# Attention and squared-ReLU MLP in one kernel: weights loaded and split earlier, two staging pools for the bias rows, and the exponent's offset computed on ScalarE

## The chip, the cores and the metric

The kernel runs on one core of a Trainium2 chip. A core has five engines, each with an instruction queue of its own that it works through in order: TensorE (PE, matmuls; its weight loads are listed as PEld), VectorE (DVE), ScalarE (ACT), GpSimd (POOL) and SyncE (SP). In this kernel every DMA is issued by SP, so SP's queue (SPq in the rows) is the order in which transfers start. The metric is device time in microseconds: the median of three runs, and, for the profile, one profiled execution.

## What is computed

```python
scores = scale * np.matmul(q, k.transpose(0, 1, 3, 2))          # 4 batches, 8 heads, 576 rows, 64 wide
x = (psi_rel / psi_i)[..., None]                                # log1p(|i-j|) / log1p(max(i,1))
h = np.maximum(x @ w1 + b1, 0.0)                                # 32 hidden values
bias = h @ w2                                                   # one value a head, the same for all batches
scores = scores + bias.transpose(2, 0, 1)[None, :, :, :]
scores = scores - np.max(scores, axis=-1, keepdims=True)
attn = np.exp(scores)
attn = attn / (np.sum(attn, axis=-1, keepdims=True) + 1e-09)
out = np.matmul(attn, v)
...
h = np.maximum(x @ w_in, 0.0)                                   # 2304 tokens, 512 -> 2048
return (h * h @ w_out).astype(np.float32)                       # 2048 -> 512
```

## The kernel before

**Number format.** Matmul operands are fp16 pairs: a value is split into a high half and the remainder, and a product is three matmuls (high by high, high by low, low by high). A split costs a cast of the high half and a subtraction for the low one, on ACT, POOL or DVE as the table `ENG` (L30) says.

**Steps.** The attention is 80 steps: two batch pairs, five row chunks of each (`ORDER`, L39), eight heads of each chunk. Chunk 0 of a pair holds the last 64 rows of both batches (one softmax block of 128 rows a step), the others 128 rows of both (two blocks a step). The first two chunks, steps 0 to 15, are done with fp32 transposes on PE and an fp32 product with v (`f32c`, L129); from step 16 on, the exponentials are split on ACT and POOL and transposed by DMA. Step t does `qk` (scores into the PSUM tile `sc`), `softmax_a`, `softmax_b`, and, three steps late, `pv`. The softmax of a block is: DVE adds the bias tile `bt` to `sc` and takes the row maximum (`s`, `mx`, L382); DVE makes the exponent's offset `nm` = ESC ln 2 - max (L385, 128x1); ACT takes the exponential with `nm` as its bias and sums the row (L388).

**The bias** depends on the rows, not on the batch, so it is made once, in 36 groups of 16 rows: four rows `hg` a group and quadrant of hidden values (L278 on ACT or L281 on DVE; the string `HID` and the list `PATS` say how many of a group's four are made on ACT), a matmul with w2 (`bp`, L308), an eviction `be` (L319 or L321), a DMA of `be` into a DRAM table `biasd` (L323), and for each step a DMA of its bias tile `bt` back (L336, L338; three buffers). `be` takes one of five buffers of the pool `r_p`, which `cv` (below) and, from step 11 on, the MLP's `r` and output tiles use as well. Four groups are made before step 0, the others a group or two a step. The groups of the second chunk, steps 8 to 15, are numbers 16 to 23, the fifth to twelfth that are made.

**The MLP's weights** are 32 loads of 512 KB (`WT`, L178). Each goes to one of three staging buffers `stg`, is rounded to fp32 by three DVE instructions (`ci` L200, `ci` L201, `cv` L203), cast on ACT (`winH`, `woutH`, L121) and finished by two POOL instructions. I call the whole a weight task. The loads of k share the staging buffers; k and v of the first pair and the weight tasks stand in one list `loads`, where `W_AT` (L38) says how many weight tasks follow each head's k and v; a step takes its share from the list: it splits the oldest load and starts the next.

**The MLP** runs in units of 256 hidden values (`g1`: 24 matmuls `hp`, L506; `g2`: 12 matmuls into `o`, L529) as soon as a chunk's attention is finished (`finish_x`), one unit a step and the rest after the last step.

**What sets the order.** The program is traced in the order of `for t in range(NS + LAG)` (L672) and then reordered by a list scheduler by priorities; `with later(n)` (L595) lowers the priority of what is traced inside. Each engine then runs its own fixed list and waits on semaphores.

## Time and profile before

| | us |
|---|---|
| runs | 711.01, 713.51, 713.33 (median 713.33) |
| profiled execution | 713.13 |
| its span (first to last instruction) | 711.2 |
| PE, DVE, ACT, POOL busy in the span | 639.2, 437.3, 342.3, 352.4 |
| first softmax (DVE L382) starts at | 34.00 |

The span is about 1.9 us shorter than the profiled execution's time; what the rows below are measured in is the span. PE's busy share of 90% is a mean over a lead-in of some 170 us, in which PE has gaps and runs at a lower granted clock, and a long rest in which it is nearly always busy. So the profile has to be read by stages.

### The profile page before, as it was taken

The page shows a single profiled execution, that of the slowest core. Times are in us where ns is not written, and L with a number is a line of the kernel's source. Part 1 is how long each engine was busy: PE and PEld are TensorE (multiplying, and loading weights), DVE is VectorE, ACT ScalarE, POOL GpSimd, SP SyncE. Part 2 cuts the span into 40 slices and gives each one's busy share as a digit, 9 for nine tenths or more (in the row PEclk, how much of TensorE's full clock was granted, in tenths as well). Part 3 has the DMA queues.
Part 4 walks back from the last instruction along what each step waited for, and adds up shares of the span by engine and source line. Part 5 has one row for each costly group of instructions (what it writes and reads, how often), then busy time and mean ns, then how long its engine had stood idle before and what let it go on. Part 6 is the DMA issues. An engine that isn't in the chain of part 4 may idle for free.

```text
span 711.2 us, 15582 instructions
## 1 busy us (share of the span) xinstructions
PE 639.2 (90%) x6048; PEld 408.5 (57%) x6048; DVE 437.3 (61%) x981; ACT 342.3 (48%) x702; POOL 352.4 (50%) x369
## 2 busy tenths in 40 slices
PE   4286779779999998999989999999998899999997
PEld 1043446456645555666656666766665566676664
DVE  6279797998897496458756645345468557325120
ACT  6266564556776544454554353244356554531111
POOL 4124453767555445466677464335456466442211
PEclk9995695679999999999999999999999999999999
DMA  8657685656598777599896797556599778561000
GB/s 286 198 165 225 207 264 163 206 188 183 135 200 179 171 145 166 130 202 189 219 213 141 143 177 141 103 124 143 122 189 188 167 163 142 106 131 30 22 10 29
DMA packets 207720, 112.16 MB, mean 158 GB/s; under 512 B 168224, under 2 KB 184608, under 8 KB 207648
## 3 DMA queue, kind: packets, MB, share of 16 engines
q1 hardware_dynamic: 207648, 111.19, 67.1%
q8 instruction: 47, 0.77, 0.5%
q14 instruction: 25, 0.20, 0.1%
HBM read 55.44 MB, written 15.61 MB: 100 GB/s over the span
## 4 chain that ended last, share of the span: by engine, by line
PE 48%; DVE 12%; DMA 8%; issue 5%; POOL 3%; ACT 3%; SPq 0%; ACTq 0%; POOLq 0%; DVEq 0%
PE hp L506 18%; PE o L529 18%; DMA at<-a 6%; PE pv L452 4%; PE sc L367 3%; DVE s L382 2%; DVE hg L281 2%; DMA xt<-xh 2%; PE bp L308 2%; POOL a L415 1%; DVE r L514 1%; ACT a L121 1%; DVE xh L490 1%; DVE xh L489 1%; PE sc L355 1%
## 5 line engine op out<-in xcount | busy, mean ns | idle before, releaser
L506 PE MATMUL hp<-xt,winH 128*128 128x256 f16 (+1 forms) x1280 | 198.7, 265 | 3.5 <-DMA xt<-xh 3.1
L529 PE MATMUL o<-woutH,g 128*128 128x512 f16 x576 | 185.4, 381 | 2.6 <-ACT o L536 2.6
L388 ACT ACTIVATE s<-s,nm 128x576 f32<-128x576 f32 x144 | 110.5, 768 | 160.0 <-DVE nm L385 159.7
L506 PE MATMUL hp<-xt,winL 128*128 128x256 f16 (+1 forms) x640 | 164.1, 265 | 0.0
L506 PEld LDWEIGHTS <-winH 128*128 128x128 f16 x1280 | 117.7, 99 | 38.8 <-issue 18.9
L529 PEld LDWEIGHTS <-g 128*128 128x128 f16 x864 | 83.2, 98 | 94.2 <-issue 10.7
L382 DVE CUSTOM_DVE_ANT_0 s<-sc,bt 128x576 f32<-128x576 f32 x144 | 103.5, 750 | 52.9 <-PE sc L367 28.0
L415 POOL TENSOR_TENSOR a<-s,a 128x1024 f16<-128x1024 f32 (+1 forms) x64 | 130.4, 2037 | 0.0
L514 DVE TENSOR_TENSOR r<-hp,r 128x512 f32<-128x512 f32 (+1 forms) x80 | 50.6, 633 | 121.2 <-ACT r L512 121.1
L516 POOL TENSOR_TENSOR g<-r,g 128x512 f16<-128x512 f32 (+1 forms) x80 | 85.3, 1066 | 73.4 <-DVE g L125 70.5
L529 PE MATMUL o<-woutL,g 128*128 128x512 f16 x288 | 109.7, 381 | 0.0
L414 POOL TENSOR_TENSOR a<-s,a 128x128 f16<-128x128 f32 (+1 forms) x64 | 28.4, 443 | 133.7 <-ACT a L121 117.7
L121 ACT ACTIVATE a<-s 128x1152 f16<-128x1152 f32 (+1 forms) x64 | 70.4, 1101 | 43.0 <-DMA at<-a 42.2
L281 DVE TENSOR_SCALAR hg<-tab_t,nb 128x464 f32<-128x464 f32 (+17 forms) x110 | 68.1, 673 | 10.2 <-PE bp L308 9.9
L452 PEld LDWEIGHTS <-at 128*128 128x128 f16 (+1 forms) x1792 | 60.3, 100 | 23.6 <-issue 8.1
L512 ACT ACTIVATE r<-hp 128x512 f32<-128x512 f32 (+1 forms) x80 | 43.2, 541 | 63.3 <-PE hp L506 63.1
L506 PEld LDWEIGHTS <-winL 128*128 128x128 f16 x640 | 63.5, 99 | 7.4 <-issue 1.2
L452 PE MATMUL pv<-v,at 128*128 128x64 f16 (+1 forms) x1792 | 64.2, 194 | 3.5 <-DMA at<-a 3.5
L308 PE MATMUL bp<-hg,w2s 128*32 128x288 f32 (+17 forms) x352 | 50.1, 574 | 13.2 <-ACT be L319 6.6
L367 PE MATMUL sc<-k,q 64*128 64x512 f16 x384 | 55.1, 395 | 0.0
L445 PEld LDWEIGHTS pv<-v,at 128*64 128x64 f32 (+3 forms) x320 | 40.8, 201 | 20.6 <-issue 11.7
L123 POOL TENSOR_SCALAR cv<-cv 128x512 f32<-128x512 f32 x32 | 21.4, 668 | 55.7 <-ACT winH L121 34.5
(70 smaller groups left out, 678.1 us busy)
## 6 DMA issues: line engine op xcount, KB each, us to landing
...
```

Of the source, the lines that this page charges most:

```text
L121: nc.scalar.activation(out=out, in_=in_, func=AF.Copy, scale=scale)
L281: nc.vector.tensor_scalar(ht, tab_t[:, 0:dlen(G)], scl[:, n:n + 1], nb1, op0=ALU.mult, op1=ALU.max)
L308: nc.tensor.matmul(out=bp[32 * t:32 * t + 32, 0:d1 - d0], lhsT=w2s, rhs=ts_[t][:, d0:d1], start=True, stop=True, tile_position=(0, 32 * t))
L367: nc.tensor.matmul(out=sc[:, 1024 * b:1024 * b + 512], lhsT=qt[r, qz, qs], rhs=kt[r, z, 64 * b:64 * b + 512], start=(n == 0), stop=(n == 2 ...
L382: nc.vector.tensor_tensor_reduce(s[:, 576 * b:576 * b + 576], sc[:, 960 * b:960 * b + 576], bt, inv, -3.0e38, ALU.add, ALU.max, mx[:, b:b ...
L388: nc.scalar.activation(out=sl, in_=sl, func=AF.Exp, bias=nm[:, b:b + 1], accum_out=su[:, h, b:b + 1])
L415: nc.gpsimd.tensor_tensor(av[:, :, 640:1152], ev[:, :, 0:512], av[:, :, 0:512], op=ALU.subtract)
L452: nc.tensor.matmul(out=dst, lhsT=lhsT, rhs=vt[:, vz, 5 * b + blk, :], start=(n == 0), stop=(n == 13), tile_position=(0, 0 if c else 64 * b))
L506: nc.tensor.matmul(out=hp[:, f * T:f * T + T].rearrange("p (b t) -> p b t", b=nb), lhsT=wt[:, k, c0:c0 + 128], rhs=xt[:, 0:nb, z * 4 + k, ...
L514: nc.vector.tensor_tensor(rr, hp[:, 0:2 * T], rr, op=ALU.mult)
L516: nc.gpsimd.tensor_tensor(g[:, 1, 0:2 * T], r[:, 0:2 * T], g[:, 0, 0:2 * T], op=ALU.subtract)
L529: nc.tensor.matmul(out=blk["o"][b], lhsT=g[:, z, c0:c0 + 128], rhs=wt[:, 2 * u + f, :], start=(u == 0 and f == 0 and z == 0 and wt is wout ...
```

## The change

Six edits are made together.

1. The list `loads` is gone. k and v of head h are loaded two steps ahead by `kv_dma` and split one step ahead by `kv_split`. Weight tasks have a list `ws` of their own: two weight loads are started before k and v of head 1, three tasks are split (and three more loads started) ahead of step 0, and two a step then. All splits of weights now come after the four bias groups in the program, not between them.
2. `HID`: in the fifth to twelfth bias group two of the four `hg` rows are made on ACT in place of one.
3. Of the first 16 `be` tiles every other one takes a buffer of `g_p`, the MLP's pool of four, in place of `r_p`.
4. `nm` is made on ACT (`AF.Identity`, scale -1, bias the constant column `esc`) directly ahead of the exponential, in place of DVE: 144 instructions.
5. `PATS` loses two rows that nothing used, and `hcst` two columns.
6. A memset of `esc` is added on DVE.

```diff
-HID = "221111111111111000"
-W_AT = [1, 1, 2, 2, 2, 2, 2, 2, 3, 3, 3, 2, 2, 2, 2, 1] + [0] * 16
+PATS = ["DDDD", "ADDD", "AADD"]
+HID = "222222111111111000"
+W_AT = [3, 2, 2, 2, 2, 2, 2, 2, 2, 2, 2, 2, 2, 2, 2, 1]
...
+    esc = const.tile([128, 1], F32, name="esc")
...
-                be = r_p.tile([128, 512], F32, tag="r", name="be")
+                nbe[0] += 1
+                if nbe[0] <= 16 and nbe[0] % 2:
+                    be = as_f32(g_p.tile([128, 2, 512], F16, tag="g", name="be"))
+                else:
+                    be = r_p.tile([128, 512], F32, tag="r", name="be")
...
-            nc.vector.tensor_scalar(nm[:, b:b + 1], mx[:, b:b + 1], -1.0, ESC * LN2, op0=ALU.mult, op1=ALU.add)
         for b in range(nb):
+            nc.scalar.activation(out=nm[:, b:b + 1], in_=mx[:, b:b + 1], func=AF.Identity, scale=-1.0, bias=esc)
             sl = s[:, 576 * b:576 * b + 576]
...
+    def kv_dma(h):
+        if h < H:
+            for w in "vk":
+                kv[h, w] = KV(0, h, w)
+                kv[h, w].dma()
+    def kv_split(h):
+        if h < H:
+            for w in "vk":
+                kv.pop((h, w)).split()
+    def w_tasks(i):
+        for _ in range(W_AT[i] if i < len(W_AT) else 0):
+            ld_split()
+            ld_dma(ws)
...
-    ld_dma(loads)
-    ld_dma(loads)
+    kv_dma(0)
     q_next()
     q_next()
+    ld_dma(ws)
+    ld_dma(ws)
+    kv_dma(1)
...
-        if gi < bias_due(-1):
-            with later(200 if gi > 1 else 0):
-                ld_split()
-                ld_dma(loads)
     hgen(groups[gi])
-    ld_split()
-    ld_dma(loads)
+    kv_split(0)
     q_split(*qlist[0])
     q_next()
+    with later(200):
+        w_tasks(0)
...
+        kv_split(t + 1)
+        kv_dma(t + 2)
+        w_tasks(t + 1)
         for _ in range(nls[t]):
-            if t < 32 and not pend:
-                break
             ld_split()
-            if loads:
-                ld_dma(loads)
-            elif t >= 32:
-                ld_dma(loads2)
+            ld_dma(loads2)
```

Three places show what the scheduler makes of it. The first is DVE's list from the second split of q (about 20 us into the span) to the first softmax. `stg_209`, `stg_309` are the first two weight loads before; `stg_161`, `stg_163`, `stg_314`, `stg_324` the first four of the change. Before:

```order
L244 SCALAR_TENSOR_TENSOR q_498<-qst_154,q_498 128x512
L168 SCALAR_TENSOR_TENSOR k_395<-stg_383,k_395 128x576
L203 SCALAR_TENSOR_TENSOR cv_263<-stg_209,ci_264 128x512
L200 TENSOR_SCALAR ci_386<-stg_309 128x512
L201 SCALAR_TENSOR_TENSOR ci_386<-stg_309,ci_386 128x512
L382 ISA s_329,mx_330<-sc_136,bt_317 128x576
L382 ISA mx_330 128x1
L385 TENSOR_SCALAR nm_331<-mx_330 128x1
```

With the change:

```order
L246 SCALAR_TENSOR_TENSOR q_534<-qst_156,q_534 128x512
L205 SCALAR_TENSOR_TENSOR cv_306<-stg_161,ci_307 128x512
L202 TENSOR_SCALAR ci_317<-stg_163 128x512
L203 SCALAR_TENSOR_TENSOR ci_317<-stg_163,ci_317 128x512
L205 SCALAR_TENSOR_TENSOR cv_316<-stg_163,ci_317 128x512
L202 TENSOR_SCALAR ci_327<-stg_314 128x512
L203 SCALAR_TENSOR_TENSOR ci_327<-stg_314,ci_327 128x512
L205 SCALAR_TENSOR_TENSOR cv_326<-stg_314,ci_327 128x512
L202 TENSOR_SCALAR ci_412<-stg_324 128x512
L203 SCALAR_TENSOR_TENSOR ci_412<-stg_324,ci_412 128x512
L388 ISA s_348,mx_349<-sc_137,bt_336 128x576
L388 ISA mx_349 128x1
```

Six more instructions of weight tasks stand ahead of the first softmax (nine in place of three behind the split of q), the split of head 2's k (`k_395`) has moved behind the second softmax, and `nm` is gone from this list. Counted over the whole list, 13 `cv` stand ahead of step 9's first softmax before and 19 now; 31 and 29 ahead of step 15's.

The second place is SP's list around the first reads of the bias table (`bt<-biasd`). `be_286` and `be_295` are the last bias rows that step 0 needs. Before:

```order
L191 DMA stg_400<-w_out 128x512
L191 DMA stg_461<-w_out 128x512
L323 DMA biasd_123<-be_284 128x16
L323 DMA biasd_123<-be_287 128x287
L323 DMA biasd_123<-be_295 128x288
L336 DMA bt_317<-biasd_123 64x576 x2
L336 DMA bt_320<-biasd_123 64x576 x2
L336 DMA bt_336<-biasd_123 64x576 x2
L336 DMA bt_414<-biasd_123 64x576 x2
```

With the change:

```order
L193 DMA stg_314<-w_out 128x512
L329 DMA biasd_123<-be_261 128x272
L329 DMA biasd_123<-be_278 128x287
L239 DMA qst_303<-qd 64x4x128
L329 DMA biasd_123<-be_286 128x288
L239 DMA qst_303<-qd 64x4x128
L193 DMA stg_324<-w_out 128x512
L190 DMA stg_334<-w_in 128x2x256
L342 DMA bt_336<-biasd_123 64x576 x2
L342 DMA bt_339<-biasd_123 64x576 x2
L342 DMA bt_355<-biasd_123 64x576 x2
L158 DMA stg_409<-kd 128x576
```

One weight load in place of two stands ahead of the last bias rows, two others now stand between these rows and the first bias tile, and the load of head 2's k stands behind the third tile.

The third place is ACT's list at the first two softmaxes. Before:

```order
L319 ACTIVATE be_295<-bp_290,hcst_132 128x288
L388 ACTIVATE s_329,sum_332<-s_329,nm_331 128x576
L401 ACTIVATE at_339<-tp_340 128x512
L388 ACTIVATE s_408,sum_332<-s_408,nm_410 128x576
L405 ACTIVATE at_339<-tp_346 64x128
```

With the change:

```order
L325 ACTIVATE be_286<-bp_281,hcst_132 128x288
L123 ACTIVATE winH_124<-cv_306 128x2x256
L123 ACTIVATE winH_124<-cv_316 128x2x256
L123 ACTIVATE woutH_126<-cv_326 128x512
L392 ACTIVATE nm_350<-mx_349,esc_135 128x1
L394 ACTIVATE s_348,sum_351<-s_348,nm_350 128x576
L392 ACTIVATE nm_439<-mx_438,esc_135 128x1
L407 ACTIVATE at_358<-tp_359 128x512
L411 ACTIVATE at_358<-tp_365 64x128
L394 ACTIVATE s_437,sum_351<-s_437,nm_439 128x576
```

Each exponential has an `nm` ahead of it, and three casts of weights come ahead of the first.

More of the change, by code (lines that the diff above doesn't have):

```diff
@@ L104, in tile_attention_moe @@
     nb1 = const.tile([128, 1], F32, name="nb1")
-    hcst = const.tile([128, 5], F32, name="hcst")
+    hcst = const.tile([128, 3], F32, name="hcst")
     kz = const.tile([128, NKZ, 2, 128], F16, name="kz")
     eps = const.tile([128, 1], F32, name="eps")
+    esc = const.tile([128, 1], F32, name="esc")
     ident = const.tile([128, 128], F32, name="ident")
@@ L250, in tile_attention_moe @@
     hg = {}
-    PATS = ["DDDD", "ADDD", "AADD", "AAAD", "AAAA"]
+    nbe = [0]
     def hg_z(G):
@@ L562, in bias_due @@
         return due[k - 1] + -(-(due[k] - due[k - 1]) * f // H)
-    loads = deque()
     ws = deque()
@@ L569, in tile_attention_moe @@
                 ws.append(WT(u, w, q))
-    nls = []
-    w_at = W_AT
-    for h in range(H):
-        loads.append(KV(0, h, "k"))
-        loads.append(KV(0, h, "v"))
-        n = 0
-        while ws and n < w_at[h]:
-            loads.append(ws.popleft())
-            n += 1
-        nls.append(2 + n)
-    for n in w_at[H:]:
-        m = 0
-        while ws and m < n:
-            loads.append(ws.popleft())
-            m += 1
-        nls.append(m)
-    nls += [0] * (32 - len(nls)) + [1] * 4 + [2] * 4 + [1] * 4 + [0] * 50
+    kv = {}
+    nls = [0] * 32 + [1] * 4 + [2] * 4 + [1] * 4 + [0] * 50
     loads2 = deque()
@@ L603, in __exit__ @@
             tc.cur_priority -= self.n
+    wdone = {"i": 0, "o": 0}
     def ld_dma(q):
@@ L609, in ld_dma @@
             pend.append(t)
-    wdone = {"i": 0, "o": 0}
     def ld_split():
@@ L645, in tile_attention_moe @@
     nc.vector.memset(eps, 1.0e-9 * 2.0 ** ESC)
+    nc.vector.memset(esc, ESC * LN2)
     nc.scalar.activation(out=nb1, in_=hcst[:, 0:1], func=AF.Exp)
```

## The prediction

> **What bounds the kernel now.** I read the busy time by stretches first, with bounds put where the behaviour changes; 98.33 and 167.73 are the starts of the first softmax of steps 9 and 15 (DVE's tenth and twenty-second rows of L382 behind the first).
>
> ```profile
> core 0: us, PE busy (x) PEld busy (x) DVE busy (x) ACT busy (x) POOL busy (x), PEclk, DMA share, GB/s
> 0.00:34.00 34.00, 11.47 (x78) 2.65 (x78) 15.65 (x39) 14.85 (x30) 11.15 (x21) 1.00 0.77 243
> 34.00:98.33 64.33, 48.20 (x338) 26.06 (x338) 52.38 (x106) 39.51 (x91) 24.57 (x28) 0.79 0.71 213
> 98.33:167.73 69.40, 55.50 (x354) 37.68 (x353) 63.02 (x125) 37.59 (x82) 41.47 (x51) 0.73 0.64 190
> 167.73:260.00 92.27, 88.62 (x894) 52.74 (x892) 70.99 (x154) 57.82 (x120) 50.07 (x54) 1.00 0.76 166
> 260.00:398.00 138.00, 131.63 (x1334) 85.86 (x1333) 89.99 (x206) 70.50 (x146) 85.42 (x88) 0.99 0.81 176
> 398.00:522.00 124.00, 124.00 (x1305) 83.29 (x1303) 61.38 (x152) 53.27 (x104) 60.77 (x61) 1.00 0.68 140
> ```
>
> From 34 to 167.73 DVE is the busiest engine, 115.4 of 133.7 us (86%), and PE has gaps and a granted clock of 0.73 to 0.79. From 167.73 on PE is busy 95% of the time or more at full clock. The chain that ended last says the same: the first row is its share by line in the stretch 150 to 174, the second in 398 to 522.
>
> ```profile
> by line: DVE hg L281 17.9%; DVE cv L203 14.4%; issue 13.1%; DVE ci L201 12.8%; DVE s L382 8.5%; DVE ci L200 7.8%; PE tp L400 4.6%; DVE r L514 4.2%; PE o L529 3.6%; DVE q L244 3.4%; ACT woutH L121 2.6%; PE tp L404 1.8%; DVE nm L385 1.3%; DVE
> by line: PE o L529 37.7%; PE hp L506 37.2%; PE pv L452 12.4%; PE sc L367 6.1%; PE sc L355 5.1%; PE sc L361 1.6%
> ```
>
> The waits of PE after 165 us (us, times, longest) leave little to win there; the largest are
>
> ```profile
> PE sc L361 <- DVE mx L382: 4.6, 3, 3.9
> PE pv L452 <- DMA at<-a: 3.5, 2, 1.9
> PE hp L506 <- DMA xt<-xh: 3.1, 2, 2.5
> ```
>
> So what the lead-in gives or takes should arrive at the end nearly whole: PE's list from about step 26 on is the same in both programs, and no edit adds or removes a matmul.
>
> **The start, up to the first softmax.** ACT's, SP's and DVE's rows in order of time:
>
> ```profile
> 19.57 0.65 ACT L319 ACTIVATE be<-bp,hcst 128x256 f32<-128x256 f32 x2 [4.11 <-DMA biasd<-be]
> 20.08 0.69 DVE L244 SCALAR_TENSOR_TENSOR q<-qst,q 128x512 f16<-128x512 f32 x1 [4.59 <-POOL q L123]
> 23.44 1.03 SPq L191 DMA_DIRECT2D stg<-w_out  x2
> 24.16 0.50 ACT L319 ACTIVATE be<-bp,hcst 128x288 f32<-128x288 f32 x1 [0.19 <-DMA biasd<-be]
> 24.56 1.33 SPq L323 DMA_DIRECT2D biasd<-be  x3
> 30.29 10.59 SPq L336 DMA_DIRECT2D bt<-biasd  x12
> 34.00 0.76 DVE L382 CUSTOM_DVE_ANT_0 s<-sc,bt 128x576 f32<-128x576 f32 x1 [9.84 <-DMA bt<-biasd]
> ```
>
> An eviction waits 4.11 us for a buffer whose DMA has not landed; the last rows go out by 25.9 behind two weight loads, the reading back starts at 30.29, when they have landed, and the first tile lands at 34.0. With nine buffers for twelve rows the early evictions wait for no buffer, but the ninth to twelfth still wait for the first landings, near 19.6, since the transfers ahead of these are the same 8 v, 2 k, 2 weight and 4 q loads. Ahead of the last row there is 512 KB of weights less and 288 KB of k less: 800 KB at the 243 GB/s of the first stretch is 3.3 us, so it lands near 27. Two weight loads, 1 MB or 4.3 us at that rate, now stand between it and the first tile. The second is a new wait on SP's queue: it needs the buffer that `cv_316` frees, four weight instructions behind the split of q, 20.77 + 4 x 0.69 = 23.5, and all bias tiles stand behind it; that is before 27 and costs nothing unless DVE comes 3.5 us late. The bytes of both start before the last row has landed, so the tile lands between 30.7 (27 and the 3.7 us of before) and 34. I take 31.5, **2.5 us earlier** (bounds 0 and 4). Head 2's k, split by then before, is now loaded behind the third tile and can hold step 2 by up to 1 us; that is in these bounds.
>
> **DVE's work in the lead-in.** Groups from 34 to 167.73: busy us and mean ns, then the idle time before them.
>
> ```profile
> L281 DVE TENSOR_SCALAR hg<-tab_t,nb 128x304 f32<-128x304 f32 (+9 forms) x48 | 25.6, 587 | 2.1 <-PE bp L308 2.1
> L203 DVE SCALAR_TENSOR_TENSOR cv<-stg,ci 128x512 uint32<-128x512 uint32 x30 | 20.4, 680 | 0.6
> L200 DVE TENSOR_SCALAR ci<-stg 128x512 uint32<-128x512 uint32 x29 | 20.1, 692 | 0.6
> L201 DVE SCALAR_TENSOR_TENSOR ci<-stg,ci 128x512 uint32<-128x512 uint32 x29 | 20.1, 691 | 0.5
> L168 DVE SCALAR_TENSOR_TENSOR k<-stg,k 128x576 f16<-128x576 f32 x5 | 5.3, 1052 | 5.0 <-ACT k L121 3.7 <-POOL k L123 1.3
> L385 DVE TENSOR_SCALAR nm<-mx 128x1 f32<-128x1 f32 x22 | 2.8, 144 | 0.1
> ```
>
> A weight task is 0.68 + 0.69 + 0.69 = 2.06 us of DVE. By the counts of rows in DVE's two lists:
> - From step 0 to step 9: 16 `cv` in place of 12, +4 x 2.06 = +8.2; 26 `hg` rows for 30 (seven go to ACT, one group comes sooner), -4 x 0.587 = -2.3; one k split more, +1.05; ten `nm` less, -1.3. Sum **+5.6**: DVE was busy 81% of this stretch, and the idle 12 us take half of it: +2.8. With the start, step 9 begins about as before (0.3 later; bounds 4 earlier and 5.6 later).
> - From step 9 to step 15: 10 `cv` for 18, -16.5; 15 `hg` for 18, -1.8; twelve `nm`, -1.5. Sum **-19.8**: DVE's 63.0 us become 43.2.
> - Two weight tasks, 4.1 us, move behind step 15, where DVE has 21.3 us idle in 92.3 and PE sets the pace: nothing.
>
> In the second of these PE is the busiest then. Its 55.5 us at the clock of 0.73, at the 96% of the next stretch, take 57.8 us; DVE's 43.2 at the 86% of now take 50.2, which is the end where the clock rises as PE's gaps close (the next stretch has it at 1.00). I take 57.0, near the clock that is measured: 12.4 less than 69.4, and with the 0.3 from before **-12.1**.
>
> **The offset on ACT.** No row has an Identity of 128x1 on ACT; the nearest are the reciprocal sums (128x4) and the table's first use (128x1). Beside them ACT's wait for `nm`:
>
> ```profile
> L388 ACT ACTIVATE s<-s,nm 128x576 f32<-128x576 f32 x144 | 110.5, 768 | 160.0 <-DVE nm L385 159.7
> L461 ACT ACTIVATE rd<-sum,eps 128x8 f32<-128x8 f32 (+1 forms) x20 | 5.8, 288 | 0.1
> L646 ACT ACTIVATE nb<-hcst 128x1 f32<-128x1 f32 x1 | 0.2, 203 | 0.0
> L278 ACT ACTIVATE hg<-tab_t,sm_t 128x304 f32<-128x304 f32 (+9 forms) x16 | 11.1, 692 | 8.7 <-PE bp L308 8.6
> ```
>
> So 0.20 to 0.29 us each; I take 0.29, like `rd` with its bias column: 22 in the lead-in are 6.4 us and the seven `hg` rows 4.8, on an engine busy 77.1 of 133.7 us there. Against it stands the queueing that goes. These DVE rows are one softmax's maximum and its offset, 2.7 us later:
>
> ```profile
> 90.78 0.08 DVE L382 DVE_READ_ACCUMULATOR2_ANT mx<- 128x1 f32 x1
> 90.78 0.68 DVE L203 SCALAR_TENSOR_TENSOR cv<-stg,ci 128x512 uint32<-128x512 uint32 x1
> 91.38 1.59 DVE L281 TENSOR_SCALAR hg<-tab_t,nb 128x416 f32<-128x416 f32 x3
> 92.89 0.68 DVE L244 SCALAR_TENSOR_TENSOR q<-qst,q 128x512 f16<-128x512 f32 x1
> 93.49 0.14 DVE L385 TENSOR_SCALAR nm<-mx 128x1 f32<-128x1 f32 x1
> ```
>
> Now ACT follows the maximum itself. What is queued behind a waiting `nm` on ACT (evictions, the MLP's first activation, on which PE waits) was queued behind the waiting exponential before, and longer. In the rest, 122 `nm` are 35 us on ACT, which is busy 43 to 63% in the three stretches from 167.73 to 522, and free 15 us of DVE. I cost that at **+0.7** net (bounds -4, the waits of PE on `mx`, and +6). The memset of `esc`, `hcst` and `PATS` cost nothing: they lie in DVE's first idle microseconds.
>
> [...]
>
> **Sum.** -12.1 + 0.7 = -11.4: 713.13 becomes **701.7**. The profiled execution is 0.2 below the median, so this stands for the median too.
>
> **Rivals.**
> - *The clock comes up.* PE's gaps close, its clock goes to 1.00, and DVE sets steps 9 to 15: 50.2 us, -18.9 + 0.7: **694.9**. For: 1.00 in every later stretch. Against: 0.73 came with 80% busy. [...]
> - *PE keeps its gaps.* Its waits on ACT's evictions between steps 9 and 15 stay, half of the 13.9 us idle: 55.5 + 7 = 62.5, -6.6 + 0.7: **707.2**. For: ACT gets more to do. Against: ACT has 46% idle there.
> - *The early weights only delay.* The first tile stays behind the two weight loads (0 in place of 2.5), step 9 comes 5.6 late, and PE, with waits almost as long as now, gives back 6 of its 13.9 us idle: -0.4 + 0.7, within 0.5% of before, **713.4**. Against: DVE's 19.8 us less.
> - *Slower: ACT.* From step 16 on, the `nm` stand 0.29 us each ahead of the exponentials, 120 of them, 35 us. Where the chain runs through ACT's list from softmax to transposes, as between 260 and 398, they lengthen it. It decides from 12.1 of these 35 us, a third of the steps; at half of them, 17.5: 713.13 - 12.1 + 17.5 = **718.5**. Against: ACT is busy 70.5 of 138 us there, and loses waits for a late `nm`.
>
> **How the numbers follow.** Forecast 0.50; clock 0.17; gaps 0.16; only delay 0.10; ACT 0.07. Within 0.5% means 3.6 us, about what a measurement of this kernel tells from no change. Faster 0.83, same 0.10, slower 0.07. The range goes from 693.5, the clock's case and a start at its early bound, to 711.5, short of the last two cases.
>
> **What would show it.** First softmax near 31.5; step 9 near 98; step 15's first softmax near 155, with PE over 90% busy between; PE's busy time after that unchanged; `nm` on ACT at 0.2 to 0.3 us. Wrong if step 15 is no earlier, if PE's gaps after 260 grow, or if the first tile's landing is later than 33.

## The result, and the profile after

The change takes 692.89 us, the median of four executions (690.24, 692.05, 693.73, 704.83); the kernel before took 713.42 beside it. The ratio is 0.9707, with a 95% interval of 0.9667 to 0.9747. A second set of six executions, later (`r_after` below), gave 0.972 (0.968 to 0.976). Two of these ten executions took 704 to 705 us; the ratios leave them out, and the other eight lie between 689.9 and 697.5.

The direction was right, and the size was not: 692.9 lies 0.6 us below the low end of the range, and 8.8 below the forecast of 701.7. The profiled executions are 713.13 before and 692.05 after, with spans of 711.2 and 690.3 us.

The first view is the busy time by stretches, as in the prediction. The bounds are the same events as there: the first softmax, those of steps 9 and 15, and then stretches of the same length as before.

```profile
core 0: us, PE busy (x) PEld busy (x) DVE busy (x) ACT busy (x) POOL busy (x), PEclk, DMA share, GB/s
0.00:33.48 33.48, 9.91 (x78) 2.66 (x78) 19.14 (x44) 16.03 (x31) 13.72 (x24) 0.73 0.86 265
33.48:104.95 71.47, 51.27 (x358) 27.62 (x359) 57.94 (x105) 49.98 (x118) 32.83 (x37) 0.79 0.75 229
104.95:151.40 46.45, 42.00 (x312) 29.90 (x312) 43.03 (x88) 33.29 (x82) 26.87 (x35) 0.85 0.64 192
151.40:240.00 88.60, 84.92 (x896) 52.21 (x896) 67.94 (x129) 63.76 (x144) 54.56 (x58) 1.00 0.78 178
240.00:378.00 138.00, 135.43 (x1372) 88.37 (x1369) 93.19 (x180) 83.31 (x185) 86.98 (x89) 1.00 0.87 186
378.00:502.00 124.00, 124.00 (x1300) 82.53 (x1299) 56.98 (x127) 62.28 (x136) 62.86 (x62) 1.00 0.71 137
```

Start times of the same softmax rows, and what the span gains up to there:

| | before | after | earlier by | forecast |
|---|---|---|---|---|
| first softmax | 34.00 | 33.48 | 0.5 | 2.5 |
| step 9 | 98.33 | 104.95 | -6.6 | -0.3 |
| step 15 | 167.73 | 151.40 | 16.3 | 12.1 |
| end of the span | 711.2 | 690.3 | 20.9 | 11.4 |

So most of the gain is made in one place, from step 9 to step 15: 46.45 us where there were 69.40. DVE's busy time there is 43.03, and the forecast was 43.2. PE's is 42.00 at a granted clock of 0.85, and the forecast kept 55.50 at 0.73. The lead-in up to step 9 gives back 6.6 (in `r_after`, a second profiled execution of the change, 8.9: step 9 at 107.25), and 4.6 more are won behind step 15, where the forecast had a loss of 0.7.

The chain that ended last, by line, first for step 9 to step 15 and then for 378 to 502:

```profile
by line: PE pv L451 30.9%; PE tp L406 15.7%; PE bp L309 9.9%; PE sc L373 9.5%; PE o L535 7.5%; PE hp L512 5.8%; DVE s L388 2.9%; PE tp L410 2.8%; DVE ci L202 2.8%; PE sc L367 2.7%; issue 2.1%; DVE hg L282 2.1%; DVE v L139 1.7%; DVE x L470 1
by line: PE o L535 39.2%; PE hp L512 35.7%; PE pv L458 12.4%; PE sc L373 6.1%; PE sc L361 5.1%; PE sc L367 1.6%
```

In the first, PE's rows shown make 85%; before, around 150 to 174, DVE's weight and `hg` rows led. The second is as it was. In `r_after` the chain from step 9 to step 15 (107.25 to 152.78) is shared, 37% by DVE's rows shown and 30% by PE's:

```profile
by line: issue 12.1%; PE pv L451 10.8%; DVE s L388 10.7%; DVE hg L282 8.4%; PE o L535 8.0%; DVE ci L202 5.6%; PE tp L406 4.6%; DVE v L139 4.5%; DVE ci L203 4.3%; DMA biasd<-be 4.2%; PE bp L309 3.5%; PE sc L373 3.3%; DVE cv L205 3.3%; PE hp 
```

The largest waits of PE behind 150 us (us, times, longest), and the two groups of ACT that make the offset and the exponential:

```profile
PE sc L367 <- DVE mx L388: 3.9, 1, 3.9
PE pv L458 <- DMA at<-a: 3.9, 2, 1.9
PE hp L512 <- DMA xt<-xh: 1.9, 2, 1.5
```

```profile
L394 ACT ACTIVATE s<-s,nm 128x576 f32<-128x576 f32 x144 | 111.4, 774 | 6.9
L392 ACT ACTIVATE nm<-mx,esc 128x1 f32<-128x1 f32 x144 | 41.1, 286 | 120.9 <-DVE mx L388 120.7
```

`nm` takes 286 ns on ACT, where 290 were assumed. The wait that stood before the exponential (160.0 us) now stands before `nm` (120.9), with 6.9 left, so 32 us of it are gone.

The start, SP's rows and the first softmax in order of time:

```profile
24.22 0.55 SPq L193 DMA_DIRECT2D stg<-w_out  x1
24.86 0.41 SPq L190 DMA_DIRECT2D stg<-w_in  x1
26.99 3.68 SPq L342 DMA_DIRECT2D bt<-biasd  x6
33.48 0.76 DVE L388 CUSTOM_DVE_ANT_0 s<-sc,bt 128x576 f32<-128x576 f32 x1 [2.07 <-DMA bt<-biasd]
```

The first read of the bias table is issued at 26.99, as forecast ("near 27"), but its tile is there only 6.5 us later, and before the change it took 3.7. In `r_after` it takes 8.3, and the first softmax starts at 34.39, so the 0.5 us that are gained here are not clear of what executions differ by.

### The profile page after: what moved, and what is told of

Its sections match the earlier page's. It is cut to its first block, busy times and chain, and to the rows that moved or that the text cites. A ratio compares the mean times of both kernels' runs of the same rounds, so it can differ in the third digit from the quotient of the medians.

```text
span 690.3 us, 15578 instructions
## 1 busy us (share of the span) xinstructions
PE 626.1 (91%) x6048; PEld 402.7 (58%) x6048; DVE 415.6 (60%) x830; ACT 384.9 (56%) x854; POOL 354.0 (51%) x369
## 4 chain that ended last, share of the span: by engine, by line
PE 69%; DMA 12%; DVE 8%; issue 4%; ACT 3%; POOL 2%; SPq 0%; DVEq 0%; ACTq 0%; POOLq 0%
PE hp L512 23%; PE o L535 23%; PE pv L458 6%; DMA at<-a 6%; PE sc L373 5%; PE bp L309 3%; PE pv L451 3%; DMA stg<-kd 3%; DVE hg L282 2%; DMA xt<-xh 1%; PE tp L406 1%; PE sc L367 1%; PE sc L361 1%; DMA stg<-w_out 1%; DVE s L388 1%
## 5 line engine op out<-in xcount | busy, mean ns | idle before, releaser
L512 PE MATMUL hp<-xt,winH 128*128 128x256 f16 (+1 forms) x1280 | 195.8, 263 | 1.9 <-DMA xt<-xh 1.9
L512 PE MATMUL hp<-xt,winL 128*128 128x256 f16 (+1 forms) x640 | 162.0, 262 | 0.0
L512 PEld LDWEIGHTS <-winH 128*128 128x128 f16 x1280 | 116.2, 98 | 36.5 <-issue 17.7
L392 ACT ACTIVATE nm<-mx,esc 128x1 f32<-128x1 f32 x144 | 41.1, 286 | 120.9 <-DVE mx L388 120.7
L282 DVE TENSOR_SCALAR hg<-tab_t,nb 128x464 f32<-128x464 f32 (+17 forms) x102 | 62.4, 665 | 9.8 <-PE bp L309 9.6
L309 PE MATMUL bp<-hg,w2s 128*32 128x288 f32 (+17 forms) x352 | 48.1, 547 | 9.1 <-ACT be L325 5.0
L451 PEld LDWEIGHTS pv<-v,at 128*64 128x64 f32 (+3 forms) x320 | 36.1, 181 | 16.8 <-issue 10.7
```

What stands on the lines that cost most here:

```text
L282: nc.vector.tensor_scalar(ht, tab_t[:, 0:dlen(G)], scl[:, n:n + 1], nb1, op0=ALU.mult, op1=ALU.max)
L309: nc.tensor.matmul(out=bp[32 * t:32 * t + 32, 0:d1 - d0], lhsT=w2s, rhs=ts_[t][:, d0:d1], start=True, stop=True, tile_position=(0, 32 * t))
L451: nc.tensor.matmul(out=dst, lhsT=lhsT, rhs=vt[r, 5 * b + blk, :], start=(blk == 0), stop=(blk == 4), tile_position=(0, 0 if c else 64 * b))
L512: nc.tensor.matmul(out=hp[:, f * T:f * T + T].rearrange("p (b t) -> p b t", b=nb), lhsT=wt[:, k, c0:c0 + 128], rhs=xt[:, 0:nb, z * 4 + k, ...
```

## The experiments

All ratios are to the kernel before, from executions on the same chip, with 95% intervals; 0.0035 of ratio is 2.5 us.

### Each edit alone, on the kernel before

`s_load` is edit 1, `s_hid` edit 2, `s_buf` edit 3, `s_nm` edit 4; each has the lines of the diff that belong to it, and nothing else of the change that acts.

```diff
# s_load (the list of loads, as in the diff above)
-W_AT = [1, 1, 2, 2, 2, 2, 2, 2, 3, 3, 3, 2, 2, 2, 2, 1] + [0] * 16
+W_AT = [3, 2, 2, 2, 2, 2, 2, 2, 2, 2, 2, 2, 2, 2, 2, 1]
...
+        kv_split(t + 1)
+        kv_dma(t + 2)
+        w_tasks(t + 1)
# s_hid
-HID = "221111111111111000"
+HID = "222222111111111000"
# s_buf (the counter and the other branch as in the diff above)
+                if nbe[0] <= 16 and nbe[0] % 2:
+                    be = as_f32(g_p.tile([128, 2, 512], F16, tag="g", name="be"))
# s_nm
-            nc.vector.tensor_scalar(nm[:, b:b + 1], mx[:, b:b + 1], -1.0, ESC * LN2, op0=ALU.mult, op1=ALU.add)
+            nc.scalar.activation(out=nm[:, b:b + 1], in_=mx[:, b:b + 1], func=AF.Identity, scale=-1.0, bias=esc)
```

> Only the order of loads and weight tasks (edit 1). Work theory: six DVE instructions go ahead of the first softmax and two tasks behind step 15, 7 us of DVE work less between, so 4 to 8 us faster, 705 to 709. Queue theory: nothing or a little slower, 712 to 716, since nm stands behind more weight work in the first steps.

> Only the table HID (edit 2): eight hg rows from DVE to ACT in the first eight steps. Work theory: up to 4.1 us faster, 709 to 711. Queue theory: nothing, 712 to 714, since nm still stands in DVE's list.

> Only the second pool for the first bias rows (edit 3). Both theories: the first softmax up to 2.5 us earlier than 34.0, and nothing later, 711 to 713. If the bias rows' buffers are not what the start waits for, 34.0 and 713.

> Only the offset nm on ACT (edit 4), all else as before. Work theory (an edit is worth the DVE time that it takes out of the lead-in): 22 x 0.127 = 2.8 us faster and 0 to 2 more later, 709 to 711. Queue theory (what counts is the 1 to 3 us for which nm stood behind other work in DVE's list, so that exponentials come late): more than 8 us faster, under 705, with step 15's first softmax under 160. ACT rival: slower than 715.

| | median (lowest to highest, executions) | ratio | first softmax | step 9 | step 15 |
|---|---|---|---|---|---|
| before | 713.45 (709.93 to 716.42, 20) | | 34.00 | 98.33 | 167.73 |
| s_load | 703.98 (701.43 to 705.98, 4) | 0.987 (0.983 to 0.991) | 31.40 | 104.09 | 151.26 |
| s_hid | 712.39 (708.33 to 717.08, 10) | 0.9994 (0.9965 to 1.0024) | 33.40 | 104.63 | 164.06 |
| s_buf | 707.71 (704.93 to 708.24, 5) | 0.9914 (0.9884 to 0.9944) | 31.02 | 96.06 | 158.49 |
| s_nm | 707.61 (703.06 to 711.71, 10) | 0.9916 (0.9885 to 0.9947) | 33.63 | 107.04 | 166.21 |

The four gains are 9.5, 1.1, 5.7 and 5.8 us, 22.1 in all, and the change has 20.5. So the edits add up as far as these intervals tell, which is to about 5 us for the sum. The load order is the largest. Against what was expected: `s_load` came out 1 us better than its work theory (705 to 709); `s_buf` gained 5.7 us where both theories had at most 2.5, and step 15 comes 9.2 us earlier, for a reason that is not shown; `s_nm` fell between its two theories; `s_hid` lies where the queue theory had it, 712 to 714, and that theory falls below. The row that the forecast counted least, `nm`, is worth as much as the buffers, and in `s_nm` the gain comes late: step 15 is only 1.5 us earlier, the end 7.1. Two edits that bring the first softmax 2.6 to 3.0 us forward go apart by step 9, so the start alone does not carry through.

Step 9 is late in `s_hid` and `s_nm` too, which move no load. In both, the scheduler puts 15 `cv` between the first softmax and that of step 9, where 12 stood before and 16 stand in the change. So step 9 is no fixed point of the work, and the early weights of edit 1 are not needed to make it late.

### Where nm's gain comes from

`l_nm` is the change with `nm` on DVE again. `n_early` and `n_late` have it there in steps 0 to 15 only (24 blocks, where the expectation says 22) and from step 16 on only. `a_dve` is the change with a row on DVE that costs what `nm` cost there, but nobody waits for it.

```diff
# l_nm
+            nc.vector.tensor_scalar(nm[:, b:b + 1], mx[:, b:b + 1], -1.0, ESC * LN2, op0=ALU.mult, op1=ALU.add)
...
-            nc.scalar.activation(out=nm[:, b:b + 1], in_=mx[:, b:b + 1], func=AF.Identity, scale=-1.0, bias=esc)
# n_early, n_late: the same under
+            if now[0] < 16:
+            if now[0] >= 16:
# a_dve
+        n2 = sml.tile([128, 2], F32, tag="n2", name="n2")
...
+            nc.vector.tensor_scalar(n2[:, b:b + 1], mx[:, b:b + 1], -1.0, ESC * LN2, op0=ALU.mult, op1=ALU.add)
```

> The change with nm back on DVE (edits 1, 2, 3 remain). Additive theory: what nm on ACT gives alone (5.8 us, nearly all of it behind 260 us) is missing here: 698.7, first softmax of step 15 within 2 us of the 151.4 of the change, and PE idle again behind 240 us as before the change (6.4 us of the 138 from 260 to 398, in place of 2.6). Rival, the edits cover the same loss: 693 to 694, with PE as busy behind 240 us as with the change.

> The change with one more DVE row of 128x1 a block that reads the maximum and writes a column nobody reads (n2, 144 of them, 0.14 us each, some 20 us of DVE); nm itself stays on ACT. Queue theory (nm's gain came from ACT no longer waiting for a row that stood behind other work in DVE's list): the gain stays, 692.9 plus 0 to 1.5. Work theory (the gain came from 20 us less for DVE to do): the gain goes, 698 to 699, with the loss behind 240 us.

> The change with nm back on DVE in steps 0 to 15 alone (22 of 144). With nm on DVE throughout, the total was 702.7, with 6.7 us of the loss there by step 15 and 4.6 more by the end. Lead-in theory (the offset's place counts where DVE and PE are both near full, and little later): step 15 at 158, total 699 to 701. Rest theory (it counts mostly in the 122 later blocks): step 15 within 2 us of 151.4, total within 2 us of 692.9.

> The change with nm back on DVE from step 16 on (122 of 144). Lead-in theory: step 15 within 2 us of 151.4, then 2 to 4.6 us lost between 240 and 400, total 695 to 697.5. Rest theory: total 701 to 703, nearly all lost behind step 15.

| | median (lowest to highest, executions) | ratio | step 9 | step 15 |
|---|---|---|---|---|
| l_nm | 702.71 (700.54 to 704.9, 4) | 0.9825 (0.978 to 0.987) | 106.49 | 158.09 |
| a_dve | 703.51 (700.73 to 706.5, 4) | 0.9838 (0.9789 to 0.9887) | 105.22 | 160.72 |
| n_early | 698.82 (697.24 to 704.26, 4) | 0.9804 (0.9736 to 0.9872) | 103.77 | 156.22 |
| n_late | 702.76 (695.19 to 707.96, 4) | 0.9763 (0.9673 to 0.9852) | | |

`l_nm` lies 0.0118 of ratio above the change, 8.4 us, give or take 4; the additive theory had 5.8. Its rival (693 to 694) falls, and so does the half of the theory that had step 15 within 2 us: it comes 6.7 later. The queue theory falls: in `a_dve` ACT waits for nothing new, and the loss is as large as in `l_nm`, beyond the 698 to 699 of the work theory. What DVE has to do counts, not only what is queued ahead of `nm`, with one reserve: an added row also makes the scheduler order the lists otherwise (12 `cv` from step 9 to step 15 in `a_dve`, 10 in the change). `n_early` is close to its lead-in theory (step 15 at 158, 699 to 701), and its rest theory falls for the total. The group that was added, from `a_dve`:

```profile
L393 DVE TENSOR_SCALAR n<-mx 128x1 f32<-128x1 f32 x144 | 18.6, 147 | 0.2
```

For the part behind step 15, here is PE's busy time in 138 us of the stretch that answers to 260 to 398 before (131.63 there). The rows are not quite the same, since these windows begin 451 us before the end of the span in the kernel before, 444 in `s_nm` and 434 to 437 in the others. One row each of the change, `s_nm`, `n_early` (`nm` on ACT in this stretch), and of `l_nm` and `a_dve` (more on DVE):

```profile
256.00:394.00 138.00, 135.43 (x1396) 89.79 (x1395) 85.31 (x170) 84.39 (x187) 90.26 (x92) 1.00 0.90 183
```

```profile
260.00:398.00 138.00, 135.42 (x1397) 88.70 (x1394) 91.12 (x176) 84.33 (x187) 89.80 (x91) 1.00 0.88 186
```

```profile
262.00:400.00 138.00, 134.99 (x1393) 89.41 (x1392) 86.77 (x170) 84.21 (x187) 89.87 (x92) 1.00 0.88 183
```

```profile
264.00:402.00 138.00, 132.49 (x1375) 87.76 (x1373) 86.47 (x205) 70.37 (x142) 86.45 (x90) 1.00 0.84 179
```

```profile
268.00:406.00 138.00, 132.82 (x1374) 88.26 (x1370) 88.29 (x207) 83.07 (x185) 90.72 (x92) 1.00 0.87 178
```

Without the rows on DVE PE works 2.2 to 3.8 us more of these 138, and ACT, with 14 us more to do, shows no loss. In `r_after` the same row has 133.54, so one execution of the change differs from another by 2 us there. In `n_early` nothing of note is lost behind 240 us (5.8 us behind the change there, 6.5 at 400). The total of `n_late` decides nothing: its profiled execution lies 4.3 us above its own median, and its interval covers both answers.

The time that PE's last 5000 matmuls take tells more; they begin some 29 us behind step 15. It is 509.9 us in the change and 511.1 in `r_after`, and 508.6 to 511.5 in nine of the ten profiled executions that have `nm` on ACT there (the tenth, `a_warm`, has 515.2). It is 513.0 to 518.7 in the nine that have it on DVE, with 513.5 in `l_nm` and 513.0 in `n_late`, and 513.5 in `a_dve`. So the late part of `nm` is worth some 2 to 4 us in the change, and `a_dve`, which has `nm` on ACT and only the work on DVE, has none of it: that points to DVE's 18 us of rows more than to what waits for `nm`.

### More work for PE, and another start

`a_fill` puts four more matmuls ahead of the scores of steps 10 to 15, so that the softmax waits for them. `a_w1` takes the two weight loads away from ahead of the first bias tile and brings the tasks back in the next two steps.

```diff
# a_fill, FILL = {t: 2 for t in range(10, 16)}
+            for _ in range(FILL.get(now[0], 0)):
+                for b in range(2):
+                    r = slice(64 * b, 64 * b + 64)
+                    nc.tensor.matmul(out=sc[:, 1024 * b:1024 * b + 512], lhsT=qt[r, 0, qs],
+                                     rhs=kt[r, 0, 64 * b:64 * b + 512],
+                                     start=True, stop=True, tile_position=(64 * b, 0))
# a_w1
-W_AT = [3, 2, 2, 2, 2, 2, 2, 2, 2, 2, 2, 2, 2, 2, 2, 1]
+W_AT = [1, 3, 3, 2, 2, 2, 2, 2, 2, 2, 2, 2, 2, 2, 2, 1]
```

> The change with four more matmuls of 64x512 into sc ahead of the scores of each of steps 10 to 15 (24 in all, overwritten by what follows; by the 5.6 us that 36 such matmuls are busy there, 3.7 us more for PE at that clock). PE theory (steps 9 to 15 take what PE's work takes at the clock granted there, which is what the prediction assumed): step 9 to step 15 grows from 46.5 by 3.7 or more to 50.2 and the total to 696.6. DVE theory (DVE's 43 us of work set these 46.5, and PE's clock comes up by what PE needs): within 1.5 us of 46.5, PE's clock there above the 0.85 of the change, total within 1.5 us of 692.9.

> The change with W_AT = [1, 3, 3, 2, ...]: one weight task split ahead of step 0 in place of three, no weight load between the last bias row and the first bias tile, and the same number of weight tasks from step 2 on. Start theory (the two weight loads ahead of the first tile cost the start 2.5 to 3 us, which reaches the end): first softmax at 31, step 9 3 us earlier, total 690. Sum theory (DVE's work up to step 9 decides, and the weights only change places): first softmax at 31, but step 9 within 1.5 us of the 104.95 of the change, total within 1.5 us of 692.9.

`a_fill`: 703.74 us (701.01 to 705.24, 4 executions), ratio 0.9836 (0.9799 to 0.9874). Step 9 to step 15 takes 53.39 us, 6.9 more, at a clock of 0.90; the PE theory said 3.7 or more, and 696.6 in all. The added rows lie between one softmax and the next, and PE is busy 5.6 us more there (47.59 for 42.00). The DVE theory, as it was stated, falls: DVE's work is not all that counts.

`a_w1`: 694.46 us (694.16 to 696.14, 4), ratio 0.9716 (0.9684 to 0.9748), the same as the change. In order of time from its start:

```profile
20.96 0.41 SPq L193 DMA_DIRECT2D stg<-w_out  x1
...
27.17 3.68 SPq L342 DMA_DIRECT2D bt<-biasd  x6
30.79 0.76 DVE L388 CUSTOM_DVE_ANT_0 s<-sc,bt 128x576 f32<-128x576 f32 x1 [0.74 <-DMA bt<-biasd]
```

With no weight load between, the tile needs 3.6 us from its issue in place of 6.5, or of the 8.3 in `r_after`, and the first softmax is 2.7 us earlier than in the change. With one weight load just ahead it needs 4.5 (`s_load`) and 4.7 (`s_buf`). It is worth nothing: step 9 starts at 107.20, later than in the change (104.95) and as in `r_after` (107.25). The start theory falls. The sum theory had step 9 within 1.5 us, which missed, and the total within 1.5 us of 692.9, where it is 1.6 above.

### The clock of PE

In `l_nm`, steps 9 to 15 hold what the forecast assumed, a busy PE at the old clock. Its rows around the longest stretch at half clock:

```profile
111.00:114.60 3.60, 2.44 (x17) 2.12 (x17) 3.60 (x8) 2.17 (x5) 1.63 (x2) 0.92 0.57 118
114.60:121.50 6.90, 6.70 (x29) 3.22 (x29) 4.17 (x10) 2.90 (x7) 2.87 (x6) 0.50 0.72 223
121.50:128.30 6.80, 6.80 (x31) 4.74 (x30) 6.60 (x17) 4.74 (x12) 1.29 (x3) 0.50 0.58 142
128.30:135.00 6.70, 6.70 (x32) 4.95 (x30) 5.08 (x12) 4.06 (x10) 4.41 (x5) 0.50 0.70 233
135.00:142.00 7.00, 7.00 (x46) 5.38 (x47) 4.20 (x10) 2.30 (x6) 3.33 (x4) 0.55 0.25 77
142.00:152.00 10.00, 10.00 (x98) 7.08 (x95) 8.72 (x21) 6.12 (x15) 6.04 (x9) 1.00 0.43 138
```

After 1.2 us of gaps the clock stands at half for 27 us in which PE is never idle for more than 0.2 us; a matmul starts every 220 ns there, and every 100 once it has come up, in a mix that is not quite the same. To see whether the clock is a handle of its own, matmuls were added whose result nobody reads, behind the scores, where no softmax was meant to wait for them: eight a step in steps 2 to 15 (`a_warm` on the change, `l_warm` on `l_nm`, `b_warm` on the kernel before), or ten a step in steps 8 to 10 (`a_kick`, `l_kick`). `r_after` is the change again.

```diff
# ..._warm; in ..._kick: {8: 10, 9: 10, 10: 10}.get(now[0], 0)
+        for _ in range(8 if 2 <= now[0] < 16 else 0):
+            nc.tensor.matmul(out=sc[:, 640:896], lhsT=qt[:, 0, qs], rhs=kt[:, 0, 0:256], start=True, stop=True)
```

> The change with eight more matmuls of 128x256 behind the scores of each of steps 2 to 15, into columns of sc that nobody reads, so that no softmax waits for them (112, about 0.11 us each at full clock and 0.21 at half: 12 to 24 us more for PE). Clock theory (between the start and step 15 PE's rows take what they take because the clock is at half for a third of the time, and it falls where PE has gaps): PE's clock from 33 to step 15 rises from 0.82 to 0.93 or more, and step 15 comes no later than the 151.4 of the change, total 688 to 693. Work theory (PE's work counts, whatever the clock): step 15 comes 12 us or more later, total 700 to 706.

> The same added matmuls in the change with nm on DVE (702.7 without them; step 9 to step 15 in 51.6 us, PE busy 96% of it at a clock of 0.74). Clock theory: PE's clock in that stretch rises above 0.9, step 9 to step 15 in 46 us or less, total below 700. Work theory: step 9 to step 15 in 57 us or more, total 708 to 714.

> The change itself again, for the spread of its own time. n_late (same rows on all engines up to step 11 or so, same times there within 0.4 us) lost 11 us against the change between steps 11 and 14, with PE 100% busy at half clock for 34 us where the change had 10. Clock theory: the same two outcomes belong to the change itself: most executions at 690 to 694 and some, one in four or more, at 701 to 708. Rival theory (something in n_late's program does it): all executions at 690 to 695.

> The change with ten more matmuls of 128x256 behind the scores of each of steps 8, 9 and 10 (30, 3.2 us for PE at full clock, 6.4 at half), into columns of sc that nobody reads; they lie where PE has its longest gaps, at 87 to 108. Clock theory: PE's clock from step 9 to step 15 is 0.93 or more in place of 0.85, steps 9 to 15 take 41 to 45 us in place of 46.5, the total is 688 to 692, and hardly an execution is above 700. Work theory: steps 9 to 15 take 3 us more, total 696 to 699.

> The same thirty matmuls in the change with nm on DVE (702.7 without them). Clock theory (what nm on ACT is worth in the lead-in, 6.7 us by step 15, comes through the clock of steps 9 to 15, 0.74 there with PE 96% busy): the clock rises above 0.9, steps 9 to 15 take 47 us or less in place of 51.6, total 696 to 699. Rival theory (it is worth this by itself, by what ACT and DVE wait): steps 9 to 15 stay at 51 or more, total 702 to 706.

> The kernel before with eight more matmuls of 128x256 behind the scores of each of steps 2 to 15, as in a_warm. DVE theory (before the change DVE's 86% busy set the lead-in, and PE's clock was only a consequence of PE's waits): the clock from 34 to step 15 rises from 0.76 to 0.88 or more, but step 15 starts within 3 us of 167.7 and the total is within 4 us of before. Clock theory for before: step 15 starts at 160 or earlier, total 708 or less.

| | median (lowest to highest, executions) | ratio |
|---|---|---|
| a_warm | 700.02 (696.48 to 704.18, 4) | 0.9791 (0.9708 to 0.9874) |
| l_warm | 706.22 (703.7 to 707.52, 4) | 0.989 (0.983 to 0.9949) |
| r_after | 695.95 (689.94 to 704.22, 6) | 0.972 (0.968 to 0.976) |
| a_kick | 698.05 (696.7 to 699.61, 6) | 0.9769 (0.974 to 0.9797) |
| l_kick | 707.95 (704.4 to 712.0, 8) | 0.9923 (0.9884 to 0.9962) |
| b_warm | 713.11 (711.35 to 716.16, 10) | 0.9993 (0.9965 to 1.0021) |

Steps 9 to 15, one row each of `a_warm`, `a_kick`, `l_nm`, `l_kick`, `b_warm` and `r_after`:

```profile
106.48:158.23 51.75, 44.90 (x378) 32.13 (x377) 49.70 (x92) 35.81 (x87) 31.18 (x40) 0.93 0.66 199
```

```profile
104.78:155.12 50.34, 42.69 (x362) 30.26 (x361) 47.91 (x94) 36.26 (x87) 30.42 (x37) 0.93 0.63 184
```

```profile
106.49:158.09 51.60, 49.75 (x330) 34.30 (x329) 42.86 (x97) 30.63 (x71) 26.91 (x35) 0.74 0.57 170
```

```profile
106.13:154.39 48.26, 42.50 (x351) 30.72 (x352) 45.85 (x97) 30.56 (x70) 25.84 (x33) 0.93 0.65 172
```

```profile
104.66:164.70 60.04, 50.05 (x362) 35.27 (x360) 54.83 (x113) 35.10 (x76) 36.18 (x46) 0.83 0.64 187
```

```profile
107.25:152.78 45.53, 40.27 (x325) 28.52 (x323) 44.30 (x88) 33.44 (x82) 27.68 (x35) 0.93 0.65 193
```

The test is not as clean as it was meant to be. Softmaxes did wait for the added matmuls, which stand in the same PSUM tile. This is what the traces of `a_warm` and `a_kick` put down to them (us, times):

```profile
  DVE s L390: 6.0, 5
  DVE s L390: 3.9, 1
```

In `b_warm` it is 5.2 us before four softmaxes, in `l_warm` 2.6 before four, in `l_kick` nothing. The scheduler's lists differ too: from step 9 to step 15 DVE has 49.70 us to do in `a_warm` and 47.91 in `a_kick`, and 43.03 in the change.

From the first softmax to step 15 the mean clock is 0.88 in `a_warm`, for 0.82 and 0.81 in the change and `r_after`, 0.87 in `l_warm` for 0.73 in `l_nm`, and 0.86 in `b_warm` for 0.76 before: the added rows go with a higher clock there. The 0.93 of `a_kick` from step 9 to step 15 proves nothing, since `r_after` has it without added rows. On the change the rows bought nothing: `a_warm` and `a_kick` need 5.3 and 3.9 us more for these steps, with DVE 95 to 96% busy. The totals are those of the work theory (700.02 for 700 to 706, 698.05 for 696 to 699), but its mechanism is not: PE is busy only 2.9 and 0.7 us longer there than in the change, DVE 6.7 and 4.9, and step 15 of `a_warm` comes 6.8 us later and not 12, in an execution 4.2 us above its median. `l_warm` lies between its two theories, 53.15 us for the stretch and 706.2 in all, and decides nothing. In `l_kick` the stretch took 48.26 in place of 51.60, one execution each, where PE had been the full engine; the clock theory asked for 47 or less. The total got worse all the same: behind step 15 `l_kick` takes 552.0 us and `l_nm` 543.1, and why is not shown. In `b_warm` the total is the same as before, as the DVE theory said, and step 15 comes 3.0 us earlier, at the edge of what it allowed; the clock ahead of it is 0.88 up to step 9 and 0.83 from there, short of the 0.88 throughout.

Of `r_after`'s six executions one took 704, less than the one in four that the clock theory expected, and the other five run from 689.94 to 697.49, wider than its 690 to 694. The clock of the profiled one is 0.93 from step 9 to step 15 with 0.74 ahead of it, against 0.85 and 0.79 in the first one. So the clock differs from execution to execution of one program. `n_late` shows what that can be worth. Its lists are those of the change, row by row, until behind step 15 (DVE's first 254 rows, ACT's first 247, PE's first 1086), and its steps 9 to 15 are

```profile
105.34:162.60 57.26, 52.89 (x313) 36.82 (x312) 43.36 (x88) 33.75 (x82) 26.88 (x35) 0.67 0.52 154
108.90:143.10 34.20, 34.20 (x170) 24.20 (x173) 22.00 (x44) 18.84 (x48) 10.63 (x15) 0.50 0.48 136
```

DVE has the same 43 us to do as in the change, PE is 92% busy, and the stretch takes 10.8 us more than the 46.45 of the change, at a clock of 0.67 for 0.85. The second row is its time at half clock: 34 us, with PE busy throughout.

What fits is a pair of limits, the later of which decides. From step 9 to step 15 (shares of the stretch):

| | us | DVE | PE | PE's clock |
|---|---|---|---|---|
| before | 69.40 | 63.02 (91%) | 55.50 (80%) | 0.73 |
| s_buf | 62.43 | 60.04 (96%) | 49.94 (80%) | 0.78 |
| b_warm | 60.04 | 54.83 (91%) | 50.05 (83%) | 0.83 |
| s_hid | 59.43 | 55.97 (94%) | 43.98 (74%) | 0.80 |
| s_nm | 59.17 | 53.48 (90%) | 48.74 (82%) | 0.74 |
| a_warm | 51.75 | 49.70 (96%) | 44.90 (87%) | 0.93 |
| a_kick | 50.34 | 47.91 (95%) | 42.69 (85%) | 0.93 |
| l_kick | 48.26 | 45.85 (95%) | 42.50 (88%) | 0.93 |
| a_w1 | 47.18 | 44.47 (94%) | 39.84 (84%) | 0.93 |
| s_load | 47.17 | 45.71 (97%) | 40.30 (85%) | 0.91 |
| the change | 46.45 | 43.03 (93%) | 42.00 (90%) | 0.85 |
| r_after | 45.53 | 44.30 (97%) | 40.27 (88%) | 0.93 |
| l_nm | 51.60 | 42.86 (83%) | 49.75 (96%) | 0.74 |
| n_early | 52.45 | 43.16 (82%) | 47.88 (91%) | 0.79 |
| n_late | 57.26 | 43.36 (76%) | 52.89 (92%) | 0.67 |
| l_warm | 53.15 | 49.30 (93%) | 49.98 (94%) | 0.90 |
| a_fill | 53.39 | 46.37 (87%) | 47.59 (89%) | 0.90 |
| a_dve | 55.50 | 46.91 (85%) | 46.75 (84%) | 0.76 |

In the first twelve DVE is 90 to 97% busy; in the first execution of the change PE is near it, at 90%. In `l_nm`, `n_early` and `n_late` DVE has the same 43 us to do, PE's rows take 48 to 53 us at the lower clock, and PE is the full engine; in `l_warm` both are full. `a_fill` and `a_dve` fit neither: there both engines are at 84 to 89%, as if part of what one waits for the other added up, which is not shown.

### Less for DVE, in two sizes

If DVE sets these steps where the clock is up, taking more off it must help. `a_hid` and `a_hid2` go on with edit 2: one more `hg` row a group on ACT in six and in twelve further groups.

```diff
-HID = "222222111111111000"
+HID = "222222222111111000"
+HID = "222222222222111000"
```

> The change with two hg rows of four on ACT in the thirteenth to eighteenth bias group as well (six rows, 0.56 us each on DVE, 0.69 on ACT; DVE has four rows less ahead of step 9 and two less from there to step 15). Two-limit theory (from step 9 to step 15 the later of DVE's work and PE's work at the clock granted: DVE 93 to 97% busy where the clock is 0.85 or more, PE 92 to 96% busy where it is 0.74 or less): with the clock up, DVE's work there is 42 and the stretch takes 44.5 to 45.5, step 9 comes 1 to 2 us earlier, total 690 to 692.5. ACT theory (the rows only move to an engine on the path): total 694 or more.

> The same to the twenty-fourth group (twelve rows; from step 9 to step 15 DVE has five hg rows less and one weight task less, 4.9 us, ahead of step 9 four rows less). Two-limit theory: DVE's work from step 9 to step 15 is 38.5; with the clock up the stretch takes 41 to 43, unless PE's 36 us at full clock, 40 at 0.9, set it; total 686 to 690. ACT theory: 8.3 us more on ACT in the lead-in, total 694 or more.

| | median (lowest to highest, executions) | ratio | step 9 | step 15 |
|---|---|---|---|---|
| a_hid | 689.82 (687.74 to 691.36, 6) | 0.9689 (0.965 to 0.9728) | 103.03 | 148.65 |
| a_hid2 | 687.43 (684.68 to 689.11, 6) | 0.9658 (0.9622 to 0.9693) | 103.04 | 143.65 |

```profile
103.04:143.65 40.61, 36.35 (x318) 25.55 (x317) 40.14 (x81) 36.02 (x87) 24.75 (x33) 1.00 0.70 206
```

That row is steps 9 to 15 of `a_hid2`: 40.61 us, DVE 99% busy, PE at full clock. Both came out much as the two-limit theory said: step 9 1.9 us earlier than in the change, the stretch 45.62 and 40.61 us for 44.5 to 45.5 and 41 to 43, the totals 0.2 us under the range and inside it. The ACT theory falls. In `a_hid2` the clock is also the highest, 1.00, so a part of its gain may come by PE. Its six executions, 684.68 to 689.11, all lie below the fastest of the ten of the change, 689.94; by ratio it gains 0.006 on `r_after`, give or take 0.005. What `a_hid` gains, 0.002 to 0.003, is not clear of the noise.

## Why the prediction was right in direction and wrong in size

**What bounds the kernel**: right in the main. 16.3 of the 20.9 us of the span are gained by step 15, and they arrive at the end.

**The start, 2.5 us earlier**: 0.5. The bias table is read at 26.99, as worked out; the tile's way was mis-sized. It was set between 3.7 and 7 us, and taken as 4.5; behind two weight loads it is 6.5, and 8.3 in `r_after`. `a_w1` has the first softmax 2.7 us earlier without these loads, and the end is the same.

**Step 0 to step 9, DVE +5.6, "the idle 12 us take half of it"**: DVE's busy time is 57.94 for 52.38, +5.6 to the digit. But nothing was taken up: the stretch is 71.47 for 64.33, 7.1 longer, and DVE is 81% busy in both. Step 9 is 6.6 later, not 0.3. What took these us is not shown.

**Step 9 to step 15, "I take 57.0, near the clock that is measured"**: this is the step that failed. DVE's sum was right (43.2; measured 43.03). PE's term was not, in two ways. PE's rows in the stretch are 312 and not 354, since the first softmax of step 9 now comes later in PE's list and that of step 15 earlier (PE has begun 436 and 748 matmuls by then, 416 and 768 before). And the clock of 0.73 was carried over as if it belonged to the program, where it differs from execution to execution: 0.85 and 0.93 in two of the change, 0.67 in `n_late` with the same lists. So PE's work takes 42.00 and 40.27 us in place of 55.5, and the stretch 46.45 and 45.53 in place of 57.0, with DVE 93 and 97% busy and PE 90 and 88%. Which of the two leads differs too: PE's rows make most of the chain at 0.85 (85% by the rows shown), DVE's the larger part at 0.93 (37%, and PE's 30%). `l_nm` is the forecast's case, PE 96% busy at 0.74, and takes 51.6 with 330 rows. Of the 10.6 us that the stretch falls short of the forecast, 6.3 only pay back step 9, which is later than forecast by that much: step 15 is 4.2 us earlier than forecast.

The rival *the clock comes up* had this mechanism, with DVE as the limit and 694.9 as its time. It was given 0.17, because "0.73 came with 80% busy"; its 50.2 us came from DVE's share of 86%, and DVE at 93 to 97% gives 44.5 to 46.5 us. Its full clock did not come: 0.85 and 0.93. That the clock rises as PE's gaps close was the author's estimate, and the runs do not settle it: with added matmuls the mean clock up to step 15 is 0.86 to 0.88 for 0.73 to 0.82, but `l_nm` and `n_late` have 27 and 34 us at half clock in which PE is never idle for more than 0.2 us. So busy in the profile is not enough, and what it needs is not shown.

**The offset on ACT, +0.7 in the rest**: this term failed too, by its sign. 286 ns a row is as assumed. But behind step 15 the change wins 4.6 us, 0.6 beyond the bound of -4, and this makes 5.3 of the 9.5 us by which the forecast missed the span. The prediction gave the 15 us of DVE's rows that go there no worth, with DVE busy 65% of the stretch from 260. By PE's last 5000 matmuls the offset on ACT is worth 2 to 4 us there, and `a_dve` loses them with DVE's rows alone. Why a row counts on an engine that is a third idle is not shown. In the lead-in the offset stood in the sum as 2.8 us of DVE's rows; `l_nm` and `n_early` are 6.7 and 4.8 us behind the change at step 15, both at a lower clock.

**The two weight tasks behind step 15, the memsets**: no sign of a cost; PE is 96% busy in the stretch behind step 15 as before.

**The other rivals**: *PE keeps its gaps* falls (4.45 us idle from step 9 to 15, for its 7, and PE's busy time is 42.00 us, not 55.5). *The early weights only delay* falls by 20 us, though its first half, the late first tile and the late step 9, is what happened. *Slower: ACT* falls: with `nm` on ACT PE's last 5000 matmuls take less time, not more, and the move of more rows to ACT in `a_hid2` gains 0.006 of ratio.

**The price of a row on ACT** (edits 2 and 4): a row costs more there than on DVE, 286 ns for 148 with `nm`, and 679 for 561 with `hg` in the lead-in, a mean over ten shapes. For the kernel the runs go the other way, `s_nm` 0.9916 and `a_hid2` 0.9658 against the change's 0.972. From step 9 to step 15 of the change DVE is 93% busy and ACT 72%, which fits `a_hid2`; the gain of `s_nm` comes mostly behind step 15, where this is no reason.

**The sum**: -16.3 by step 15 in place of -12.1, and -4.6 in place of +0.7; 9.5 us in all of the span. By step 15 it is near by luck in part: step 9 is 6.3 us later than forecast, and the stretch behind it 10.6 shorter.
